# Another order for the attention turns that carry no side products: a difference of scores through ScalarE in place of one maximum in eight

## The chip, the cores and the metric

The kernel runs on one core of a Trainium2 chip. Five engines work side by side on it, each through its own list of instructions in order: TensorE (PE in the profile; its weight loads stand apart as PEld), VectorE (DVE), ScalarE (ACT), GpSimd (POOL) and SyncE (SP), which issues most transfers. Matrix products end in PSUM, eight banks of 128 partitions by 512 numbers; VectorE and ScalarE read them from there. The metric is the time of one execution on the device in microseconds; lower is better.

## What is computed

The reference is a block with a modulated layer norm, attention with 32 query heads that share one key and one value head of 16 columns, and a gated product of two projections without a nonlinearity:

```python
x = A_x
mod = (_silu(c) @ w_mod).reshape(c.shape[0], 6, 1, -1)
sa, ca, ga, sb, cb, gb = (mod[:, 0], mod[:, 1], mod[:, 2], mod[:, 3], mod[:, 4], mod[:, 5])
h = _layernorm(x, axis=-1) * (1 + ca) + sa
q = (h @ wq) in 32 heads of 16; k = h @ wk; v = h @ wv        # one key and one value head
p = _softmax(q @ k.T / 4, axis=-1)
x = x + ga * ((p @ v) @ wo)
h = _layernorm(x, axis=-1) * (1 + cb) + sb
x = x + gb * (((h @ w_gate) * (h @ w_up)) @ w_down)
```

There are 2048 rows of 512 columns, and the gated part is 1792 wide. Everything is float32 outside; inside, products that need it are made of two float16 halves.

## The kernel before

The attention is cut into 32 *units*. A unit is one block of 512 query rows and four heads, so `u = 8 * block + group` (`UB = 8`). For each unit the largest score of every query row is wanted before the exponentials are taken, and so each unit is worked on twice.

*Maxima.* The maxima of unit u are taken while unit u-1 is in its exponentials. They come in 32 slots, each with one product for `a = 0` and one for `a = 1`: 128 queries against 512 of the 2048 keys, into a PSUM tile `mx`. The two values of `a` are two heads that stand in the upper and the lower 64 rows of TensorE's array (48 of the 64 are used), so two such products with different `a` can stream at the same time. VectorE reduces each `mx` to one column of `mpart` (L574). After slot 31 `max_fin` reduces `mpart` to `mm` (L591), TensorE transposes `mm` into `mxt` (L598), ScalarE and VectorE write it as two halves `mt` (L603, L604), and two transfers lay these as two more rows into `sst`, the query operand of the unit. A score that comes out of `sst` and `kst` then already has its maximum taken off.

*Exponentials.* A *turn* is one tile of 128 keys of a unit, 16 turns to a unit. It has four products `sc` (keys by 512 queries, four heads, by `p` and `a`; L621), four exponentials on ScalarE into `P` (L623), and the product P times V of the turn before it (`pv`, L632): four products with 128 rows and 32 columns each, side by side in the array, whose sums stay in one PSUM bank for the whole unit. `P` has eight buffers, two turns' worth.

*PSUM.* All eight banks stand in one queue. `ps_hold` takes the one at the front, `ps_give` puts it at the end, and `ps_mx` and `ps_sc` do both at once. `pv` holds one bank for good, so a tile `mx` or `sc` gets the bank of the seventh tile before it, and its product waits until ScalarE or VectorE has read that tile. Anything else that is placed between turns (the transposes `mxt`, sums of squares of weights at L916, transposes of the second layer norm at L765) takes a bank from the same queue.

*Side products.* Projections of q, the output projection and the gated part are cut into groups of products, and each turn takes some of them in between where a group is ready. `attend` makes two turns and chooses one of three orders for both (written by hand, as strings): `MANY` (eight side products a turn), `FEW` (four a turn, for q) and `NO_SIDE`. In a string, `e0` is a score product with its exponential for `a = 0`, `m1` a maximum for `a = 1`, `x0` a side product. `NO_SIDE` stands where no side product is to be had. By the program these are 31 calls of `attend`, two turns each: 26 in one stretch, from unit 5, turn 6, to unit 8, turn 9, while maxima of units 6 to 9 are taken; and 5 from unit 9, turn 8, to unit 10, turn 1, while the block's second layer norm is made ready (maxima of units 10 and 11).

After the products of a turn `attend` calls `pv` for the turn before. In the middle and at the end of each turn it runs what stands in lists: `late_max` (the transpose of a unit's maxima, a slot after `max_fin`), `hooks` (weight loads, splits and sums of squares; a step of these lists is half a turn), `turns` (the transposes L765), and at the start and in the middle `drain_posts`, the evacuations that belong to what was run before.

*The first unit.* For unit 0, where nothing else keeps VectorE busy, another form of the maximum is there already. Of two 512-key parts a and b, TensorE makes b - a in one bank, as two products (`kng` is a part of the keys with its sign turned); ScalarE takes its positive part into `rel` (L577); then TensorE makes a, and one VectorE instruction adds `rel` and reduces the sum to its maximum (L579, with a short second instruction that reads the accumulator). That is the maximum over both parts.

Of the kernel before, what the change touches and what calls it, by code (L numbers as in the profile page):

```python
# [23 lines left out]
UB = H // 4  # L24
NU = NB * UB
KT = S // 128
# [13 lines left out]

CHANNEL = {0: KC - 1, 3: 0, 4: 1, 6: 2}
LOW = -3.0e38
SYNC = mybir.DependencyInfo(mybir.DependencyClass.Sync, mybir.DependencyReason.DATA)

NO_SIDE = "e0 e1 m0 m1 e0 e1 m0 m1"
FEW = "e1 m0 e0 x1 m0 x1 e0 x1 m0 x1 e1 m0"  # L50
MANY = "x1 e0 x1 m0 x1 e0 x1 e0 x1 m0 x1 m0 x1 m0 x1 e0"

# [2 lines left out]
def adaln_mqa_glu_kernel(ctx: ExitStack, tc: tile.TileContext, x_in, wq_in, wk_in, wv_in, wo_in,  # L55
# [410 lines left out]
    ended = []  # L466
# [72 lines left out]
    def max_slots(u):  # L539


        if u == 0:
            slots = [[[("one", r // 4, r % 4, kc)] for _ in range(2)] for kc in range(2) for r in range(8)]
            for r in range(8):
                for a in range(2):
                    slots[-1][a].append(("diff", r // 4, r % 4, 2))
                slots.append([[("both", r // 4, r % 4, 2)] for _ in range(2)])
            return slots
        return [[[("one", r // 4, r % 4, kc)] for _ in range(2)] for kc in range(4) for r in range(8)]

    flat = [(u, i, last, step) for u in range(NU) for steps in [max_slots(u)]
# [4 lines left out]
    def max_parts(u):  # L556
        if u < NU and u not in mparts:
            mparts[u] = work.tile([128, 2, 2, 4, 4], F32, name="mpart")
            if u == 0:
                nc.vector.memset(mparts[u], LOW)  # L560

    def max_mm(u, a, op):
# [19 lines left out]
    def drain_relus():  # L582
        for f in relus:
            f()
        relus.clear()
# [41 lines left out]
    def pv(u, kt):  # L627
        if kt == 0:
            pvb[u] = ps_hold("pv")
        for j in range(4):  # L630
            p, a = divmod(j, 2)
            nc.tensor.matmul(pvb[u][32 * j:32 * j + 32, :], vst[:, kt, :], ptl[u, kt, p, a],  # L632
                             start=(kt == 0), stop=(kt == KT - 1))
# [413 lines left out]
    def max_half(a):  # L1047
        n = mstep[a]
        mstep[a] += 1
        if n >= len(flat):  # L1050
            return
        u, i, last, ops = flat[n]
        max_parts(u)
        for op in ops[a]:
            max_mm(u, a, op)
        if a == 0:
            return
        if 0 < u < NU - 1 and i == QPRE:
            load_q(u + 1)
        if i == 12:  # L1060
            max_parts(u + 1)
        if last:
            max_fin(u)
            (_, f, g), = max_rows(u)
            later[mstep[1] + 1] = (f, g)

    def late_max():
        for at in [m for m in later if m <= mstep[1]]:
            f, g = later.pop(at)
            f()  # L1070
            posts.append(g)
            return True
        return False
# [61 lines left out]
    def attend(u, kt):  # L1135


        now[0] = u * NSTEP + 2 * kt
        if cur and cur[0].ended():
            cur.clear()  # L1140
        side = cur[0] if cur else fill[0][1] if open_gate(now[0]) else None
        style = NO_SIDE if side is None else FEW if side in qs else MANY
        order = [(w[0], int(w[1])) for w in style.split()]
        count = {}
        for turn in range(2):
            now[0] = u * NSTEP + 2 * (kt + turn)
            sync["before"] = sync["exp"]
            drain_posts()
            for j, (what, a) in enumerate(order):
                if j == len(order) // 2:  # L1150
                    drain_posts()
                    late_max()
                    hooks(u, 2 * (kt + turn))
                a = a if style is NO_SIDE else a ^ turn
                if what == "m" and mstep[a] >= len(flat) and style is MANY:
                    mstep[a] += 1
                    side_half(a, second)
                elif what == "m":
                    max_half(a)
                elif what == "x":  # L1160
                    side_half(a)
                else:
                    k = count[a] = count.get(a, -1) + 1
                    qk_exp(u, kt + (k // 2 if style is MANY else turn), k % 2, a)
            assert not sync["due"]
            for g in ended:
                g.finish()
            ended.clear()
            for f in ends:
                f()  # L1170
            ends.clear()
            v = u * KT + kt + turn - 1
            if v >= 0:
                pv(*divmod(v, KT))
                if v % KT == KT - 1:
                    ends.append(lambda: pv_out(u - 1))
            if not late_max() and turns:
                _, f, post = turns.popleft()
                f()
                posts.append(post)  # L1180
            hooks(u, 2 * (kt + turn) + 1)
# [98 lines left out]
```

## Time and profile before

| what | before |
|---|---|
| time, median of 3 runs | 1682.76 us (1682.55 to 1683.22) |
| the profiled execution: time, span | 1682.67 us, 1680.6 us |
| granted TensorE clock | 0.998 |
| first stretch without side products, 26 pairs of turns | 299.74 to 429.17 us, 129.43 us |
| second stretch, 5 pairs | 470.25 to 499.49 us, 29.24 us |

The two stretches are measured from the start of their first exponential to the start of the first exponential after them; 208 and 40 exponentials lie in them. TensorE, VectorE and ScalarE are busy for 99%, 83% and 72% of the whole span. These shares mix stretches with side products, where TensorE is the limit, and the two without.

### The profile page before, as it was taken

How to read it: one execution, taken by the hardware profiler on the slowest of the kernel's cores; microseconds unless marked ns; L12 is line 12 of the kernel's file. 1: busy time of each engine (PE TensorE's matmuls, PEld its weight loads, DVE VectorE, ACT ScalarE, POOL GpSimd, SP SyncE). 2: the span in 40 equal slices, each digit the busy share in tenths (PEclk: the TensorE clock that was granted, in tenths of full speed). 3: DMA queues.
4: the chain of work that ended last, by engine and by line, in shares of the span. 5: the costliest groups of instructions: out<-in, count | busy, mean ns of one | idle time of the engine just before them, and what ended most of it. 6: DMA issues, size and time to landing. Idle time of an engine off the chain costs nothing.

```text
span 1680.6 us, 33352 instructions
## 1 busy us (share of the span) xinstructions
PE 1656.3 (99%) x12749; PEld 535.4 (32%) x12749; DVE 1390.0 (83%) x2365; ACT 1216.1 (72%) x2288; POOL 518.1 (31%) x690
## 2 busy tenths in 40 slices
PE   8999999999999999999999999999999999999999
PEld 3333333222223333333333333333333333334444
DVE  7999999999989999999989999999998999703110
ACT  5688888888787778777777777877777777772010
POOL 5745354626676740200140211101032111112230
PEclk9999999999999999999999999999999999999999
DMA  6112122211321200001100000000010000001000
GB/s 245 72 40 88 54 88 61 94 48 50 84 66 56 85 22 9 17 10 29 35 15 12 15 15 10 16 10 17 24 32 12 23 16 6 12 5 49 13 1 25
DMA packets 48556, 66.33 MB, mean 39 GB/s; under 512 B 14726, under 2 KB 29194, under 8 KB 48396
## 3 DMA queue, kind: packets, MB, share of 16 engines
q1 hardware_dynamic: 46812, 63.87, 12.2%
q8 instruction: 100, 1.64, 0.4%
q14 instruction: 60, 0.49, 0.1%
q10 hardware_dynamic: 1584, 0.33, 0.1%
HBM read 51.05 MB, written 8.65 MB: 36 GB/s over the span
## 4 chain that ended last, share of the span: by engine, by line
PE 87%; DVE 9%; ACT 2%; DMA 1%; issue 0%; ACTq 0%; DVEq 0%
PE side L485 50%; PE pv L632 27%; DVE mpart L574 8%; PE sc L621 5%; PE mx L570 3%; ACT P L623 2%; PE mx L765 1%; DMA xbig<-in_A_x_dram 1%; PE mxt L598 0%; DVE bs L238 0%; PE sc L570 0%; PE pk L274 0%; DMA wkv<-in_A_wv_dram 0%; DVE rel L579 0%; PE part L267 0%
## 5 line engine op out<-in xcount | busy, mean ns | idle before, releaser
L574 DVE TENSOR_REDUCE mpart<-mx 128x1 f32<-128x512 f32 x2016 | 1266.1, 683 | 91.6 <-PE mx L570 88.3
L623 ACT ACTIVATE P<-sc 128x512 f32<-128x512 f32 x2048 | 1092.0, 599 | 264.6 <-PE sc L621 223.1
L621 PE MATMUL sc<-sst,kst 50*128 50x512 f16 x2048 | 661.0, 379 | 1.0 <-DVE mpart L574 0.8
L570 PE MATMUL mx<-kst,sst 48*128 48x512 f16 x2032 | 617.3, 377 | 6.5 <-DVE mpart L574 3.8
L632 PE MATMUL pv<-P,vst 128*32 128x512 f32 x4096 | 545.3, 605 | 1.2
L485 PE MATMUL side<-h2T,wg 64*128 64x512 f16 (+1 forms) x1168 | 284.3, 378 | 0.1
L485 PE MATMUL side<-h2T,wu 64*128 64x512 f16 (+1 forms) x1166 | 282.9, 378 | 0.1
L485 PE MATMUL side<-wd,glu 64*128 64x512 f16 (+1 forms) x1008 | 234.1, 378 | 0.0
L818 POOL TENSOR_SCALAR glu<-gf 128x512 f16<-128x512 f32 x56 | 34.7, 620 | 617.2 <-DVE gf L817 538.9
L621 PEld LDWEIGHTS <-kst 50*128 50x128 f16 x2048 | 175.2, 94 | 129.4 <-issue 109.6
L570 PEld LDWEIGHTS <-sst 48*128 48x128 f16 x2064 | 183.9, 94 | 58.7 <-issue 37.4
L485 PEld LDWEIGHTS <-wg 64*128 64x128 f16 (+1 forms) x1168 | 100.9, 94 | 202.7 <-ACT P L623 95.0
L485 PEld LDWEIGHTS <-wu 64*128 64x128 f16 (+1 forms) x1166 | 100.8, 95 | 200.2 <-ACT P L623 92.5
L632 PEld LDWEIGHTS pv<-P,vst 128*32 128x32 f32 x4096 | 80.8, 108 | 218.8 <-issue 202.8
L485 PEld LDWEIGHTS <-glu 64*128 64x128 f16 (+1 forms) x1008 | 89.1, 95 | 163.2 <-ACT P L623 63.0
L817 DVE TENSOR_TENSOR gf<-side,g 128x512 f32<-128x512 f32 x56 | 38.3, 684 | 115.8 <-PE side L485 82.5
L485 PE MATMUL side<-h,wq 64*128 64x512 f16 (+1 forms) x349 | 92.5, 376 | 0.0
L812 ACT ACTIVATE g<-side 128x512 f32<-128x512 f32 x56 | 33.2, 593 | 81.5 <-PE side L485 81.5
L485 PE MATMUL side<-wo,och 64*128 64x512 f16 (+1 forms) x336 | 79.3, 378 | 0.0
L819 POOL TENSOR_TENSOR glu<-gf,glu 128x512 f16<-128x512 f32 x56 | 65.0, 1161 | 4.7
L200 POOL TENSOR_SCALAR rv<-st 128x1 f32<-128x1 f32 (+1 forms) x20 | 4.6, 228 | 158.3 <-DVE st L725 143.2
L666 POOL TENSOR_TENSOR oc<-oc,rr 128x512 f32<-128x512 f32 x15 | 19.1, 1275 | 107.4 <-DMA sst<-qd 94.3
(223 smaller groups left out, 810.5 us busy)
## 6 DMA issues: line engine op xcount, KB each, us to landing
wsl<-in_B_w_gate_dram SPq DMA_DIRECT2D x32, 224.0 KB
wsl<-in_B_w_up_dram SPq DMA_DIRECT2D x32, 224.0 KB
wsl<-in_B_w_down_dram SPq DMA_DIRECT2D x28, 256.0 KB
sst<-qd SPq DMA_DIRECT2D x180, 32.0 KB
oc<-ev SPq DMA_DIRECT2D x128, 32.0 KB
rr<-ri SPq DMA_DIRECT2D x16, 256.0 KB
xl<-in_A_x_dram SPq DMA_DIRECT2D x16, 256.0 KB
qd<-q SPq DMA_DIRECT2D x15, 256.0 KB
```

The source lines that it names most:

```text
L485: return nc.tensor.matmul(self.p, left[64 * r0:64 * r1], right[64 * r0:64 * r1], start=start, stop=self.ended())
L570: nc.tensor.matmul(m, s[64 * a:64 * a + 48, p, t * 128:(t + 1) * 128], w[64 * a:64 * a + 48, :], start=(i == 0), stop=(i == len(keys) - 1))
L574: nc.vector.tensor_reduce(part, m, axis=AX.X, op=OP.max)
L621: nc.tensor.matmul(t, kst[64 * a:64 * a + 50, kt * 128:(kt + 1) * 128], s[64 * a:64 * a + 50, p, :], start=True, stop=True)
L623: ex = nc.scalar.activation(ptl[u, kt, p, a], t, AF.Exp)
L632: nc.tensor.matmul(pvb[u][32 * j:32 * j + 32, :], vst[:, kt, :], ptl[u, kt, p, a], start=(kt == 0), stop=(kt == KT - 1))
L666: eng.tensor_tensor(o, o, st["r"], op=OP.mult)
L765: nc.tensor.transpose(st["p"][:, t * 128:(t + 1) * 128], n2s[b, t][:, k * 128:(k + 1) * 128], ident)
L812: nc.scalar.activation(st["g", f], p, AF.Copy, scale=2.0 ** -45)
L817: nc.vector.tensor_tensor(gf, p, st["g", f], op=OP.mult)
L818: nc.gpsimd.tensor_scalar(st["glu"][:, 0, f, :], gf, 1.0, 0.0, op0=OP.mult, op1=OP.add)
L819: nc.gpsimd.tensor_tensor(st["glu"][:, 1, f, :], gf, st["glu"][:, 0, f, :], op=OP.subtract)
```

## The change

Three things change, and all of them in turns of the order `NO_SIDE`.

1. Units 6 to 9 (`DIFFS`) order the slots of their maxima by row instead of by key part, `a = 0` taking the parts in the order 0, 2, 1, 3. In turns without side products, slot 1 of four of `a = 0` becomes a difference (parts 2 and 3, through `kng`), which ScalarE evacuates, and slot 3 becomes the product that takes `rel` along. By the program this happens 26 times, once in each pair of turns of the first stretch: VectorE gets seven tiles where it got eight, ScalarE nine where it got eight, and TensorE makes one product more. The second stretch has no differences.
2. The order is written out over two turns and changes. `a = 0` and `a = 1` no longer alternate, and the first of the two turns takes three maxima of `a = 0`, the second three of `a = 1`. A unit's last slot is therefore done when the slower of both is (`mstep[1 - a]`, `min(mstep)`).
3. `v` in the string is the place of P times V (with what the end of a turn brings, `end_turn`). In the second turn it stands ahead of the last score product.

```diff
+DIFFS = range(UB - 2, UB + 2)
+DIFF_AT, BOTH_AT = 1, 3
...
-NO_SIDE = "e0 e1 m0 m1 e0 e1 m0 m1"
+NO_SIDE = ("m0 m0 e1 m0 e1 e0 m1 e0 v", "e0 m1 m0 m1 e1 m1 e0 v e1")
...
+        if u in DIFFS:
+            order = [0, 1]
+            order[DIFF_AT:DIFF_AT] = [2]
+            order.insert(BOTH_AT, 3)
+            return [[[("one", r // 4, r % 4, kc)] for kc in (order[i], i)] for r in range(8) for i in range(4)]
...
-            if u == 0:
+            if u == 0 or u in DIFFS:
                 nc.vector.memset(mparts[u], LOW)
...
+    def max_half(a, diffs=False):
...
-        for op in ops[a]:
-            max_mm(u, a, op)
-        if a == 0:
+        for kind, p, t, kc in ops[a]:
+            if a == 0 and u in DIFFS and i % 4 == DIFF_AT and diffs:
+                kind, open_diff[0] = "diff", True
+            elif a == 0 and u in DIFFS and i % 4 == BOTH_AT and open_diff[0]:
+                kind, kc, open_diff[0] = "both", 2, False
+            max_mm(u, a, (kind, p, t, kc))
+        if mstep[1 - a] <= n:
             return
...
-            later[mstep[1] + 1] = (f, g)
+            later[min(mstep) + 1] = (f, g)
...
-        for at in [m for m in later if m <= mstep[1]]:
+        for at in [m for m in later if m <= min(mstep)]:
...
+        def end_turn(kt):
+            for g in ended:
+                g.finish()
+            ended.clear()
+            for f in ends:
+                f()
+            ends.clear()
+            v = u * KT + kt - 1
+            if v >= 0:
+                pv(*divmod(v, KT))
+                if v % KT == KT - 1:
+                    ends.append(lambda: pv_out(u - 1))
...
+            order = orders[turn]
...
-                    max_half(a)
+                    max_half(a, style is NO_SIDE)
+                    drain_relus()
+                elif what == "v":
+                    end_turn(kt + turn)
...
-            for g in ended:
-                g.finish()
-            ended.clear()
-            for f in ends:
-                f()
-            ends.clear()
-            v = u * KT + kt + turn - 1
-            if v >= 0:
-                pv(*divmod(v, KT))
-                if v % KT == KT - 1:
-                    ends.append(lambda: pv_out(u - 1))
+            if style is not NO_SIDE:
+                end_turn(kt + turn)
```

Where a pair of turns ends (`sst_128` belongs to the unit in its exponentials, `sst_126` and `sst_127` to units whose maxima are taken; `kwb` holds `kng`). On TensorE, before, around the end of a turn:

```order
L570 LDWEIGHTS sst_126
L570 MATMUL mx<-kst,sst_126 128x512
L632 MATMUL pv<-P,vst 32x512 x4
L621 LDWEIGHTS kst
L621 MATMUL sc<-sst_128,kst 128x512
L621 LDWEIGHTS kst
L621 MATMUL sc<-sst_128,kst 128x512
```

And on TensorE now, around the end of a pair's second turn, with the first products of the next pair:

```order
L628 LDWEIGHTS kst
L628 MATMUL sc<-sst_128,kst 128x512
L639 MATMUL pv<-P,vst 32x512 x4
L628 LDWEIGHTS kst
L628 MATMUL sc<-sst_128,kst 128x512
L577 LDWEIGHTS sst_127
L577 MATMUL mx<-kst,sst_127 128x512
L577 LDWEIGHTS sst_127
L577 MATMUL mx<-kst,sst_127 128x512
L628 LDWEIGHTS kst
L628 MATMUL sc<-sst_128,kst 128x512
```

A turn's last score product now stands behind `pv`, and two maxima follow it where two score products stood.

In the pair in which unit 6's last maxima are taken, TensorE before has this around the transpose `mxt` (the last slot's products stand ahead of the `pv` shown):

```order
L632 MATMUL pv<-P,vst 32x512 x4
L621 LDWEIGHTS kst
L621 MATMUL sc<-sst_128,kst 128x512
L621 LDWEIGHTS kst
L621 MATMUL sc<-sst_128,kst 128x512
L570 LDWEIGHTS sst_127
L570 MATMUL mx<-kst,sst_127 128x512
L570 LDWEIGHTS sst_127
L570 MATMUL mx<-kst,sst_127 128x512
L598 MATMUL mxt<-ident,mm 16x128
L621 LDWEIGHTS kst
L621 MATMUL sc<-sst_128,kst 128x512
```

And now:

```order
L639 MATMUL pv<-P,vst 32x512 x4
L628 LDWEIGHTS kst
L628 MATMUL sc<-sst_128,kst 128x512
L577 LDWEIGHTS sst_126
L577 MATMUL mx<-kst,sst_126 128x512
L577 LDWEIGHTS sst_127
L577 MATMUL sc<-kwb,sst_127 128x512
L577 LDWEIGHTS sst_127
L577 MATMUL sc<-kst,sst_127 128x512
L577 LDWEIGHTS sst_127
L577 MATMUL mx<-kst,sst_127 128x512
L605 MATMUL mxt<-ident,mm 16x128
```

The last slot's product (`mx` of `sst_126`) has moved from ahead of `pv` to behind it, into the same turn as the transpose that needs its reduction.

On ScalarE, before, around the evacuation `mt` of the same transpose:

```order
L638 ACTIVATE ev<-pv,evs 128x512
L623 ACTIVATE P<-sc 128x512 x16
L514 ACTIVATE qf<-side,qvs 128x512
L623 ACTIVATE P<-sc 128x512 x32
L603 ACTIVATE mt_4850<-mxt 16x128
L623 ACTIVATE P<-sc 128x512 x16
```

And now:

```order
L630 ACTIVATE P<-sc 128x512 x8
L584 ACTIVATE rel<-sc 128x512
L630 ACTIVATE P<-sc 128x512 x3
L610 ACTIVATE mt_4860<-mxt 16x128
L630 ACTIVATE P<-sc 128x512 x5
L584 ACTIVATE rel<-sc 128x512
L630 ACTIVATE P<-sc 128x512 x8
```

The positive parts stand one to eight exponentials, and ahead of `mt` are the three exponentials of the second turn, the last of them that of the score product behind `pv`.

More of the change, by code (lines that the diff above doesn't have):

```diff
@@ L1045, in drain_posts @@
             f()
-    def max_half(a):
+    open_diff = [False]
+    def max_half(a, diffs=False):
         n = mstep[a]
@@ L1053, in max_half @@
         max_parts(u)
-        for op in ops[a]:
-            max_mm(u, a, op)
-        if a == 0:
+        for kind, p, t, kc in ops[a]:
[5 more added lines that the diff above has]
+        if mstep[1 - a] <= n:
             return
+        u, i, last, ops = flat[n]
         if 0 < u < NU - 1 and i == QPRE:
@@ L1142, in attend @@
         style = NO_SIDE if side is None else FEW if side in qs else MANY
-        order = [(w[0], int(w[1])) for w in style.split()]
+        orders = [[(w[0], int(w[1:] or 0)) for w in s.split()] for s in (style if style is NO_SIDE else (style, style))]
         count = {}
+        def end_turn(kt):
[10 more added lines that the diff above has]
+                    ends.append(lambda: pv_out(u - 1))
         for turn in range(2):
```

## The prediction

> **What bounds the kernel now.** I first read where the time without side products lies (the table by stretches), then who waits there (the waits), then one turn in order of time, then the first unit, which shows the operations that are added. In the table the columns behind the length are busy time and count of TensorE, its weight loads, VectorE, ScalarE and GpSimd.
>
> ```profile
> core 0: us, PE busy (x) PEld busy (x) DVE busy (x) ACT busy (x) POOL busy (x), PEclk, DMA share, GB/s
> 299.74:429.17 129.43, 122.15 (x874) 30.38 (x872) 128.99 (x231) 109.81 (x215) 67.45 (x78) 1.00 0.21 64
> 470.25:499.49 29.24, 27.28 (x181) 7.15 (x179) 25.49 (x45) 25.88 (x50) 22.13 (x34) 1.00 0.21 63
> 333.89:338.63 4.74, 4.74 (x34) 1.11 (x32) 4.74 (x10) 4.13 (x8) 2.09 (x2) 1.00 0.35 114
> 343.39:348.17 4.78, 4.33 (x34) 1.11 (x32) 4.78 (x9) 4.13 (x8) 4.34 (x5) 1.00 0.11 31
> 394.71:400.32 5.61, 4.57 (x36) 1.03 (x33) 5.58 (x11) 4.38 (x10) 2.47 (x4) 1.00 0.00 0
> ```
>
> ```profile
> ACT P L623 <- PE sc L621: 19.2, 51, 1.1
> PE mx L570 <- DVE mpart L574: 3.8, 17, 0.2
> PE mxt L598 <- DVE mm L591: 1.9, 3, 0.8
> ```
>
> In the first stretch VectorE works 128.99 of 129.43 us. ScalarE waits 19.2 us for scores, TensorE 3.8 us for banks that VectorE has not read: both follow VectorE. A pair of turns with nothing else in it takes 4.74 to 4.78 us (the two short windows); I take 4.76. One turn:
>
> ```profile
> 339.72 12.63 DVE L574 TENSOR_REDUCE mpart<-mx 128x1 f32<-128x512 f32 x21
> ...
> 340.58 0.39 PE L621 MATMUL sc<-sst,kst 50*128 50x512 f16 x2
> ...
> 340.81 0.38 PE L570 MATMUL mx<-kst,sst 48*128 48x512 f16 x2
> ...
> 341.01 2.06 ACT L623 ACTIVATE P<-sc 128x512 f32<-128x512 f32 x4 [0.31 <-PE sc L621]
> 341.03 0.39 PE L621 MATMUL sc<-sst,kst 50*128 50x512 f16 x2
> ...
> 341.64 0.39 PE L570 MATMUL mx<-kst,sst 48*128 48x512 f16 x2 [0.23 <-DVE mpart L574]
> ...
> 341.97 1.06 PE L632 MATMUL pv<-P,vst 128*32 128x512 f32 x8
> 342.96 0.10 PEld L621 LDWEIGHTS <-kst 50*128 50x128 f16 x2 [0.84 <-issue]
> ```
>
> From it: a reduce every 0.60 us ((12.63 - 0.68) / 20), eight of them 4.78 us, which is the pair. An exponential every 0.49 us ((2.06 - 0.60) / 3). Two products of the two halves start together, and the next two 0.22 us later (340.58, 340.81, 341.03). From the last of them to `pv` it is 0.31 us (341.64 to 341.97, the second of the two a hundredth or two later), from `pv` to the next score 1.00. From a score product's start to its exponential 0.43 us. Three more delays, at places where the reader sat idle:
>
> ```profile
> 486.19 0.38 PE L570 MATMUL mx<-kst,sst 48*128 48x512 f16 x2
> ...
> 486.61 2.48 DVE L574 TENSOR_REDUCE mpart<-mx 128x1 f32<-128x512 f32 x4 [0.76 <-PE mx L570]
> ...
> 492.77 0.78 ACT L772 ACTIVATE hf<-mx,hsc 128x512 f32<-128x512 f32 x1 [0.67 <-PE mx L765]
> ...
> 493.60 0.86 PE L570 MATMUL mx<-kst,sst 48*128 48x512 f16 x2 [0.19 <-ACT hf L772]
> ```
>
> Product to reduce 0.42 us; end of the reader to the next product in its bank 0.05 (493.55 to 493.60).
>
> **The added operations** run in the first unit, before the exponentials begin:
>
> ```profile
> 57.66 0.68 DVE L579 CUSTOM_DVE_ANT_0 rel<-mx,rel 128x512 f32<-128x512 f32 x1
> 58.27 0.08 DVE L579 DVE_READ_ACCUMULATOR2_ANT mpart<- 128x1 f32 x1
> 58.27 0.69 DVE L579 CUSTOM_DVE_ANT_0 rel<-mx,rel 128x512 f32<-128x512 f32 x1
> ```
>
> ```profile
> L577 ACT ACTIVATE rel<-sc 128x512 f32<-128x512 f32 x16 | 8.4, 608 | 3.7 <-PE mx L570 2.8 <-PE sc L570 0.7
> ```
>
> The joint reduce comes every 0.61 us, its second instruction hidden inside; the positive part takes 0.61 us alone, like an exponential's 0.60, so I give it the same 0.49 in a chain.
>
> **A plain pair, now.** VectorE: 6 x 0.60 + 0.61 = 4.21 us. ScalarE: 9 x 0.49 = 4.41. TensorE without any wait: the longer row half takes four further steps of 0.22 behind the first product in each turn, so twice 0.88 + 0.31 + 1.00 = 4.38. None of the three reaches 4.76, but banks come back only after seven tiles. I follow one pair from T = 0, where the last `e1` of the pair before and the first `m0` start behind `pv`. `both` and `e1` start at 0.22, `m0` and `e1` at 0.44, `e0` at 0.66. `m1` is the seventh tile after that last `e1`, whose exponential starts at 0.43, takes 0.60 and frees the bank at 1.08; `m1` would have been ready at 0.66. The last `e0` needs the bank of the first `m0`: 0.42 + 0.68 + 0.05 = 1.15, where 0.88 would do. `pv` at 1.46, second turn at 2.46. There `e0` and `m1` start at once, the difference's two products 0.22 and 0.44 later, `e1` at 0.66, the last `m1` and `e0` at 0.88; every bank there has been free for 0.3 us or more. `pv` at 1.19, the next pair at 2.19. Sum 4.65 us: the limit passes from VectorE to TensorE and the banks, and 0.11 of the 0.55 us taken off VectorE comes through. Over 26 pairs: **-2.9 us**. Bounds: 4.38 (no bank wait, -9.9) and 4.76 (0).
>
> **VectorE's other work in the stretch** is on the limit today:
>
> ```profile
> L574 DVE TENSOR_REDUCE mpart<-mx 128x1 f32<-128x512 f32 x209 | 126.6, 677 | 0.3 <-PE mx L570 0.2
> L940 DVE TENSOR_REDUCE gm<-gbb 128x1 f32<-128x512 f32 x1 | 0.7, 662 | 0.0
> L591 DVE TENSOR_REDUCE mm<-mpart 128x16 f32<-128x64 f32 x3 | 0.7, 220 | 0.1
> ```
>
> 128.99 - 126.6 = 2.4 us, of which some 1.0 belongs to the unit ends (next). The rest, 1.4, now falls into 0.44 us a pair that VectorE has to spare; the two 0.66 reduces stick out by a little. **-1.1** (0 to -1.4).
>
> **Unit ends.** Three lie in the stretch. Before, one of them:
>
> ```profile
> 397.73 0.22 DVE L591 TENSOR_REDUCE mm<-mpart 128x16 f32<-128x64 f32 x1
> ...
> 398.10 0.27 PE L598 MATMUL mxt<-ident,mm 128*16 128x128 f32 x1 [0.81 <-DVE mm L591]
> 398.30 0.39 PE L621 MATMUL sc<-sst,kst 50*128 50x512 f16 x2
> ...
> 399.75 0.25 ACT L603 ACTIVATE mt<-mxt 16x128 f16<-16x128 f32 x1
> ...
> 400.26 0.27 DVE L604 SCALAR_TENSOR_TENSOR mt<-mxt,mt 16x128 f16<-16x128 f32 x1
> ...
> 400.48 3.72 DVE L574 TENSOR_REDUCE mpart<-mx 128x1 f32<-128x512 f32 x6
> ```
>
> TensorE waits 0.81 us for `mm`, and the pair takes 5.61 (another takes 0.2 less): about 0.75 over the plain one. Now the last slot's product stands in the turn of the transpose itself. It starts with the second turn, 2.46; its reduce runs from 2.88 to 3.56, `mm` to 3.80, `mxt` starts 0.15 later at 3.95 and the next score at 4.15, where 3.12 was due: 1.03 us. Then, in the next pair, ScalarE's `mt` queues behind the exponential of the score behind `pv`: it starts at 0.43 + 0.49 = 0.92, VectorE's `mt` at 1.22, and the pair's first reduce behind it at 1.44 in place of 0.42. The last `e0` of that turn waits for exactly this bank: another 1.02. Behind both stand `pv`, and so all. 2.05 now against 0.75: **+3.9** over three (0 if the stalls are covered as before, +5). The transfers of `mt` start about 1.5 us later in the turn; before, 3.9 us lay between the second one and the unit's first score, and the stalled pair is longer by as much, so I cost that at nothing.
>
> **Between the turns.** Four sums of squares (L916) and two small products of the weights' scales fall into the stretch:
>
> ```profile
> 352.41 0.40 PE L916 MATMUL mx<-kwb,onec 128*32 128x128 f32 x8
> 352.75 0.39 PE L621 MATMUL sc<-sst,kst 50*128 50x512 f16 x2
> ```
>
> Each takes 0.34 us of TensorE and a bank. A pair without one spares TensorE 0.38 us today (4.76 - 4.38) and nothing now. Behind the first turn such an item costs 0.3 either way; behind the second, a score stands between `pv` and it, and I add 0.2 for leaving and entering the row halves once more (2 x 0.09, the 0.31 above less 0.22). Three such: **+0.6** (0 to +2). [...] The evacuations of `pv` (three, 0.6 us of ScalarE) find 0.24 us spare a pair and stuck out by 0.2 before too: 0.
>
> **Second stretch.** No differences: VectorE keeps eight reduces, 4.78, and sits idle 0.06 at a pair's start, where the first maximum is only 0.42 behind `pv`: 5 x 0.08 = +0.4. One unit end, VectorE with more in its queue: +1.1. The four transposes, where VectorE idles 0.76 us a turn, may go either way: 0 (-1 to +1). **+1.5**.
>
> GpSimd's and SyncE's lists keep their order; GpSimd is busy 67.45 of 129.43 us, so a changed pace finds it with room. Turns with side products differ in the slots' parts alone, at no cost: TensorE limits them.
>
> **Sum.** -2.9 - 1.1 + 3.9 + 0.6 + 1.5 = +2.0 us on the profiled execution's 1682.67 (span 1680.6, 2.1 around it; the median of the runs is 1682.76): **1684.7 us**, no change that a measurement can tell (0.2% is 3.4 us). What the sum says: the gain is spent at the unit ends.
>
> **Rivals.** *Faster: banks come back in time.* If `m1` and the last `e0` are not held up, a plain pair takes 4.38 to 4.5 us, 4 to 7 us less than in my sum, and the time is 1678 to 1681; with the second stall at unit ends hidden too, 1675. For it: all three engines' sums lie below 4.41. Against: today's 0.23 us before each second pair of maxima is the same wait. It is faster by 0.2% from 0.21 us a pair below my 4.65. 0.20.
>
> *Slower: the two row halves don't overlap freely.* Today both halves start together in every step of these turns; now they start at different steps and next to others. If a product had to wait for its neighbour in the other half at two places of a pair, 0.22 us each, the pair would take 5.09 and the time is 1684.7 + 26 x 0.44 = 1696; 0.06 us a pair is enough for slower by 0.2%. Against it, in a turn with side products the halves start 0.1 us apart and keep their step (the maximum and the score are of one half, 0.23 us apart):
>
> ```profile
> 604.14 0.37 PE L570 MATMUL mx<-kst,sst 48*128 48x512 f16 x1
> ...
> 604.27 0.38 PE L485 MATMUL side<-h2T,wg 64*128 64x512 f16 x1
> 604.37 0.37 PE L621 MATMUL sc<-sst,kst 50*128 50x512 f16 x1
> ```
>
> Small delays of this kind, or unit ends at their bound of +5, are the likelier part of it: 0.32, most of it below 1690.
>
> *Table loads.* Were ScalarE to load its tables at each change between exponential and positive part, 52 loads at 1.28 us would give 1751.
>
> ```profile
> 2.29 1.28 ACT L179 ACT_TABLE_LOAD   x1 [2.29 <-issue]
> ```
>
> The one load of the program stands ahead of the first unit's positive parts and all exponentials: 0.01. [...]
>
> *It does nothing:* a transfer or GpSimd sets the time behind the stretch, 1682.8: inside my own case.
>
> **Chances and range.** My forecast, with "it does nothing" in it, 0.47; faster 0.20; slower 0.33. The range reaches into both: 1678.5 (plain pair 4.41) to 1690.5 (pair 4.85, or unit ends and items at their upper bounds).
>
> **What would show it.** In the changed kernel: plain pairs near 4.65 us with TensorE never idle for long and VectorE idle 0.4 us a pair; waits of TensorE for exponentials and reduces of some 0.3 us a pair in place of ScalarE's for scores; `mxt` waiting about 1 us for `mm`; pairs at unit ends near 5.7, twice running. Wrong if plain pairs stay at 4.76 or go below 4.5, if `mt` does not wait, or if the stretch behind 429 us shifts by another amount than these two stretches gain or lose.

## The result, and the profile after

The changed kernel takes 1680.66 us (median of 22 runs, 1679.79 to 1681.68); the kernel before, run beside it, 1683.27 (22 runs, 1682.00 to 1684.17). The ratio is 0.9986 with a 95% interval of 0.9980 to 0.9992: 2.6 us faster, a small gain where the prediction had a small loss (1684.7; its range, 1678.5 to 1690.5, holds the time). The interval leaves out 1, so the gain, though small, is there.

The table by stretches of the kernel after: the first stretch, the second, a plain pair of turns, the two pairs of a unit's end, a pair with an evacuation of `pv`. The columns are those of the prediction's first table.

```profile
300.22:427.81 127.59, 121.00 (x901) 31.56 (x900) 118.17 (x232) 119.70 (x240) 68.01 (x78) 1.00 0.22 65
468.84:498.10 29.26, 27.13 (x182) 7.45 (x182) 25.55 (x45) 26.04 (x49) 21.77 (x34) 1.00 0.22 63
389.20:393.67 4.47, 4.39 (x34) 1.17 (x33) 4.38 (x9) 4.47 (x10) 4.22 (x5) 1.00 0.06 23
393.67:399.68 6.01, 4.89 (x35) 1.12 (x34) 4.24 (x9) 4.89 (x12) 2.43 (x4) 1.00 0.01 3
399.68:404.92 5.24, 4.93 (x34) 1.26 (x34) 5.03 (x10) 4.46 (x10) 1.09 (x2) 1.00 0.44 131
404.92:409.96 5.04, 4.67 (x34) 1.20 (x33) 4.79 (x10) 5.04 (x11) 4.62 (x8) 1.00 0.01 2
```

VectorE falls from 128.99 to 118.17 us in the first stretch, ScalarE rises from 109.81 to 119.70, and the stretch is 1.84 us shorter. A plain pair takes 4.47 us, 0.29 less than the 4.76 before, and ScalarE is busy in all of it. The two pairs of a unit's end take 11.25 us where the same end took 10.35 before, 5.61 (in the prediction's table) and behind it:

```profile
400.32:405.06 4.74, 4.73 (x34) 1.11 (x32) 4.74 (x10) 4.13 (x8) 1.07 (x2) 1.00 0.47 148
```

The waits of the first stretch after, in the same view as before:

```profile
ACT P L630 <- PE mx L577: 4.7, 10, 0.9
DVE mt L611 <- ACT mt L610: 4.4, 3, 1.5
```

ScalarE's waits of exponentials for products, 19.2 us in one row before, are down to 4.7 in their largest row, and a new wait of VectorE has come: for `mt`, three times 1.5 us, at the three unit ends.

By kind of pair, from the starts of each pair's first exponential in both traces (us, after less before; "predicted" is worked out from the prediction's terms: 0.11 less in each of the 26 pairs, and what was put on top for its kind):

| pairs | count | measured | predicted |
|---|---|---|---|
| plain | 13 | -3.70 | -1.4 (13 x -0.11) |
| unit ends, two each | 6 | +3.18 | +3.2 (3.9 - 6 x 0.11) |
| with an evacuation of `pv` | 3 | +0.18 | -0.3 |
| with VectorE's other work and most of the items between turns | 4 | -1.52 | -0.9 (-1.1 - 0.4 + 0.6) |
| first stretch | 26 | -1.86 | +0.5 (-2.9 - 1.1 + 3.9 + 0.6) |
| second stretch | 5 | +0.02 | +1.5 |

The pair ahead of the first stretch is 0.25 us longer, and the pairs at the other borders of the two stretches add -0.2. Outside of these places the two profiled executions differ by 0.2 us ahead of the change and 0.4 behind it. In the kernels below, this offset ahead of the change was anywhere from 0 to 1.2 us, so it says nothing of the change.

One plain pair of the kernel after, TensorE in order of time, and one reduce of VectorE that a score waits for:

```profile
388.28 0.39 PE L628 MATMUL sc<-sst,kst 50*128 50x512 f16 x1
...
388.74 0.69 DVE L581 TENSOR_REDUCE mpart<-mx 128x1 f32<-128x512 f32 x1
...
389.40 0.37 PE L577 MATMUL mx<-kst,sst 48*128 48x512 f16 x1
389.48 0.37 PE L628 MATMUL sc<-sst,kst 50*128 50x512 f16 x1
389.79 1.07 PE L639 MATMUL pv<-P,vst 128*32 128x512 f32 x8
390.79 0.39 PE L628 MATMUL sc<-sst,kst 50*128 50x512 f16 x1
390.79 0.39 PE L577 MATMUL mx<-kst,sst 48*128 48x512 f16 x1
391.01 0.38 PE L577 MATMUL sc<-kwb,sst 48*128 48x512 f16 x1
391.01 0.38 PE L577 MATMUL mx<-kst,sst 48*128 48x512 f16 x1
391.23 0.38 PE L628 MATMUL sc<-sst,kst 50*128 50x512 f16 x1
391.23 0.37 PE L577 MATMUL sc<-kst,sst 48*128 48x512 f16 x1
391.44 0.38 PE L628 MATMUL sc<-sst,kst 50*128 50x512 f16 x1
391.45 0.38 PE L577 MATMUL mx<-kst,sst 48*128 48x512 f16 x1
391.76 1.07 PE L639 MATMUL pv<-P,vst 128*32 128x512 f32 x8
392.75 0.39 PE L628 MATMUL sc<-sst,kst 50*128 50x512 f16 x1
```

The first turn is as forecast. Its last maximum stands back until 389.40 and its last score until 389.48. The maximum starts 0.05 us behind the end of the exponential that has read its bank (388.72 to 389.35), the score 0.05 us behind the end of the reduce that has read its own (388.74 and 0.69). Then comes `pv`, and the second turn starts 2.51 us after the first (forecast: 2.46). The second turn takes 1.96 us where 2.19 was forecast. In the program the maximum at 391.01 stands behind both products of the difference (`kwb`, then `kst`), yet it starts 0.22 us ahead of the second of them (391.23). So each row half goes through its own four steps, 0.22 us apart, and neither waits for the other.

A unit's end after (all engines):

```profile
396.44 0.22 DVE L598 TENSOR_REDUCE mm<-mpart 128x16 f32<-128x64 f32 x1
...
396.81 0.27 PE L605 MATMUL mxt<-ident,mm 128*16 128x128 f32 x1 [0.73 <-DVE mm L598]
...
399.52 0.25 ACT L610 ACTIVATE mt<-mxt 16x128 f16<-16x128 f32 x1
...
399.80 0.28 DVE L611 SCALAR_TENSOR_TENSOR mt<-mxt,mt 16x128 f16<-16x128 f32 x1 [1.46 <-ACT mt L610]
```

Both forecast stalls are there. TensorE stands 0.73 us for `mm` (0.81 before, some 1 us forecast). Then VectorE stands 1.46 us, with the next pair's reduces behind, for the `mt` that ScalarE reaches only behind its exponentials (399.52, 2.7 us behind the transpose).

### The profile page after: what moved, and what is told of

The parts are those of the page before. It is cut to its first block, busy times and chain, and to the rows that moved or that the text cites. A ratio compares the mean times of both kernels' runs of the same rounds, so it can differ in the third digit from the quotient of the medians.

```text
span 1678.6 us, 33368 instructions
## 1 busy us (share of the span) xinstructions
PE 1655.8 (99%) x12775; PEld 537.8 (32%) x12775; DVE 1379.6 (82%) x2369; ACT 1225.9 (73%) x2314; POOL 518.1 (31%) x690
## 4 chain that ended last, share of the span: by engine, by line
PE 90%; DVE 5%; ACT 4%; DMA 1%; issue 1%; ACTq 0%; DVEq 0%
PE side L487 50%; PE pv L639 28%; PE sc L628 6%; PE mx L577 3%; DVE mpart L581 3%; ACT P L630 3%; PE mx L772 1%; PE sc L577 1%; DMA xbig<-in_A_x_dram 0%; PE mxt L605 0%; DVE bs L240 0%; ACT rel L584 0%; DVE rel L586 0%; PE part L269 0%; DMA wkv<-in_A_wv_dram 0%
## 5 line engine op out<-in xcount | busy, mean ns | idle before, releaser
L581 DVE TENSOR_REDUCE mpart<-mx 128x1 f32<-128x512 f32 x1964 | 1241.1, 683 | 94.0 <-PE mx L577 87.6
L628 PE MATMUL sc<-sst,kst 50*128 50x512 f16 x2048 | 686.2, 378 | 3.6 <-DVE mpart L581 1.8
L577 PE MATMUL mx<-kst,sst 48*128 48x512 f16 x2006 | 625.1, 377 | 2.8 <-DVE sst L291 0.3
L628 PEld LDWEIGHTS <-kst 50*128 50x128 f16 x2048 | 182.6, 94 | 142.3 <-issue 122.8
```

The costliest lines, as they stand in the source:

```text
L577: nc.tensor.matmul(m, s[64 * a:64 * a + 48, p, t * 128:(t + 1) * 128], w[64 * a:64 * a + 48, :], start=(i == 0), stop=(i == len(keys) - 1))
L581: nc.vector.tensor_reduce(part, m, axis=AX.X, op=OP.max)
L628: nc.tensor.matmul(t, kst[64 * a:64 * a + 50, kt * 128:(kt + 1) * 128], s[64 * a:64 * a + 50, p, :], start=True, stop=True)
```

## The experiments

All kernels are the changed kernel with one edit unless said otherwise. "Plain pair" is read from the starts of the first exponentials of successive pairs, away from unit ends, evacuations and items. The kernel before ran again beside each of them, and each ratio is to those runs.

**Parts alone.** First the differences without the new order: every turn's products as before the change.

```diff
-NO_SIDE = ("m0 m0 e1 m0 e1 e0 m1 e0 v", "e0 m1 m0 m1 e1 m1 e0 v e1")
+NO_SIDE = ("e0 e1 m0 m1 e0 e1 m0 m1 v",) * 2
```

> Differences and positive parts as in the changed kernel, but the products of every turn in the old order (scores, maxima, scores, maxima, then P times V). Theory one, the difference alone makes the gain: VectorE 4.21 us a pair, ScalarE 4.41, TensorE with free row halves 1.97 + 2.19 and one bank wait of some 0.35 behind the positive part; a plain pair takes 4.5 us (4.41 to 4.6), unit ends cost what they cost before (0.75 over a plain pair), and the time is 4 to 5 us under the kernel before, so below the changed kernel. Theory two, the new order is needed for the banks to come back in time: plain pairs at 4.65 us or more, and the time is at or above the changed kernel's.

Measured: 1683.91 us, ratio to the kernel before 1.0006 (0.9997 to 1.0015): no gain. A plain pair takes 4.82 us. The table by stretches (a plain pair), the waits in the first stretch, and TensorE in that pair:

```profile
390.75:395.57 4.82, 4.72 (x36) 1.02 (x33) 4.33 (x8) 4.51 (x11) 4.59 (x5) 1.00 0.01 4
```

```profile
DVE mpart L581 <- PE mx L577: 10.2, 24, 0.7
ACT P L630 <- PE sc L628: 9.7, 29, 0.6
```

```profile
390.96 0.85 PE L577 MATMUL mx<-kst,sst 48*128 48x512 f16 x2
...
393.19 0.38 PE L628 MATMUL sc<-sst,kst 50*128 50x512 f16 x2
393.49 0.37 PE L577 MATMUL sc<-kwb,sst 48*128 48x512 f16 x1
...
393.81 0.37 PE L577 MATMUL mx<-kst,sst 48*128 48x512 f16 x1
```

VectorE and ScalarE now both wait for products, and TensorE for banks: of the two maxima at 390.96 the second starts 0.48 us after the first instead of beside it (0.85 less 0.37), and the difference starts at 393.49, 0.30 behind the scores instead of 0.22, when VectorE gives its bank back. What ends last in both turns is one wait: the last maximum takes the bank of the turn's own first score. In the second turn shown that score starts at 392.74, its exponential runs from 393.16 to 393.76, and the maximum starts at 393.81. With the delays of the prediction this wait alone makes a turn of 0.43 + 0.60 + 0.05 + 0.31 + 1.00 = 2.39 us and a pair of 4.78, whatever VectorE does. It was there before the change too (in the turn that the prediction shows, the first score's exponential ends at 341.60 and the second of the last two maxima starts at 341.65), level with VectorE's own 4.78, so "both follow VectorE" was half of it. So "theory one" falls and "theory two" holds: VectorE's relief alone goes straight into waits for banks.

Then the new order without differences:

```diff
-DIFFS = range(UB - 2, UB + 2)
+DIFFS = range(0)
```

> The new order of products and the new place of P times V, without differences (every maximum read by VectorE). Theory one: VectorE again has eight reduces of 0.60 us a pair, so plain pairs are at 4.78 to 4.9 us; unit ends cost 2.0 us as in the changed kernel, 1 us more than before each; the time is 2 to 5 us above the kernel before. Theory two, the order itself frees time: plain pairs below 4.74 and a time at or under the kernel before.

Measured: 1690.92 us (four runs, one of them 1695.43), 1.0052 (1.0039 to 1.0066), 7.7 us above the kernel before. A plain pair:

```profile
396.45:401.35 4.90, 4.76 (x32) 1.03 (x32) 4.88 (x10) 4.17 (x10) 4.68 (x5) 1.00 0.00 0
```

The plain pair is at 4.90, at the upper end expected, with VectorE busy in 4.88 of it. The total is above the expected 2 to 5: unit ends cost 1.2 to 1.5 us more than before (I expected 1), and the four pairs with VectorE's other work lose 1.8 us, since all of it lies on the limit again.

Last, `v` alone put back to the second turn's end:

```diff
-NO_SIDE = ("m0 m0 e1 m0 e1 e0 m1 e0 v", "e0 m1 m0 m1 e1 m1 e0 v e1")
+NO_SIDE = ("m0 m0 e1 m0 e1 e0 m1 e0 v", "e0 m1 m0 m1 e1 m1 e0 e1 v")
```

> The changed kernel with P times V back at the second turn's end: its last score (e1) stands ahead of it, all else as in the changed kernel. Worked out with row halves that start products freely, signals in program order and seven banks (0.22 us a step, 0.42 to the reader, 0.49 and 0.60 between readers): that half has five steps, P times V comes 0.22 us later, and the score's exponential queues behind four others; the next turn's P times V waits for it. A plain pair takes 4.85 us, so the place of P times V is worth 0.4 us a pair and the time is some 8 to 10 us above the changed kernel's. If the place is worth nothing, plain pairs stay at 4.47 to 4.5; if only the step counts, 4.69.

Measured: 1685.97 us, 1.0017 (1.0008 to 1.0027) against the kernel before, 5.3 us above the changed kernel (expected: 8 to 10); a plain pair takes 4.90 (expected: 4.85). The expected total took the 0.4 us for every pair of the stretch; the thirteen plain pairs give 4.8 us, and the unit ends are 0.7 us shorter than the changed kernel's.

So neither the differences (+0.7 us, not told from nothing) nor the order (+7.7) gains anything by itself, nor do both without the new place of `pv` (+2.6); all together gain 2.6. The place of `pv` alone was not run.

**Do the row halves run as two lanes?** The second turn with all of the upper half's products ahead of the lower half's in the program; each half keeps its own order.

```diff
-NO_SIDE = ("m0 m0 e1 m0 e1 e0 m1 e0 v", "e0 m1 m0 m1 e1 m1 e0 v e1")
+NO_SIDE = ("m0 m0 e1 m0 e1 e0 m1 e0 v", "e0 m0 e0 m1 m1 e1 m1 v e1")
```

> The changed kernel with the second turn's products in another program order: all of the upper row half (score, the difference's two, score) ahead of those of the lower one (maximum, maximum, score, maximum); each half's own order stays. If products start in program order across the halves, as the prediction had it, the first maximum of the lower half can't start before the last score of the upper one, 0.66 us into the turn: the second turn takes 2.63 us and a plain pair 5.13, in place of 4.47 in the changed kernel. If each row half is a lane of its own that starts its products as they come, the second turn stays at 1.97 and a plain pair at 4.47 (4.41 to 4.55). If a product can pass one that waits for the other half, but only one, 4.91. The transpose of a unit's end comes to stand behind the turn's last score, so unit ends are not compared here.

Measured: 1685.5 us (one run), plain pairs 4.94 to 4.99 us and two of 5.15: on average none of the three numbers. The second turn in order of time:

```profile
394.60 0.39 PE L628 MATMUL sc<-sst,kst 50*128 50x512 f16 x1
...
394.61 0.39 PE L577 MATMUL mx<-kst,sst 48*128 48x512 f16 x1
...
395.04 0.37 PE L577 MATMUL sc<-kst,sst 48*128 48x512 f16 x1
...
395.10 0.53 PE L628 MATMUL sc<-sst,kst 50*128 50x512 f16 x2
...
395.62 1.06 PE L639 MATMUL pv<-P,vst 128*32 128x512 f32 x8
395.71 1.89 DVE L581 TENSOR_REDUCE mpart<-mx 128x1 f32<-128x512 f32 x3 [0.66 <-PE mx L577]
...
396.62 0.39 PE L628 MATMUL sc<-sst,kst 50*128 50x512 f16 x1
```

The products do run as lanes: the lower half's first maximum starts at 394.61, beside the first score, though four products of the upper half stand ahead of it in the program, three of which have yet to start, and the turn takes 2.02 us, not 2.63. But its reduce starts at 395.71, 1.10 us behind its product instead of 0.42. It starts 0.08 us behind the end of the upper half's last score (the second of the two at 395.10, which end at 395.63), the last product ahead of the maximum in the program. It is the same in each of the 26 pairs of the stretch: 0.88 us behind the difference's first product each time. So in this run products start out of order between the halves, and their readers are let go in order. The three reduces then end late, their banks come back late, and the first turns wait: 2.93 us (4.95 less 2.02) in a pair of 4.95, where it was 2.51.

To see whether the reader really hangs on the products ahead of its own, one of them is moved behind it (the edit is to the kernel just shown):

```diff
-NO_SIDE = ("m0 m0 e1 m0 e1 e0 m1 e0 v", "e0 m0 e0 m1 m1 e1 m1 v e1")
+NO_SIDE = ("m0 m0 e1 m0 e1 e0 m1 e0 v", "e0 m0 m1 e0 m1 e1 m1 v e1")
```

> As in the run with the upper half's products ahead, but the first maximum of the lower half stands ahead of the upper half's last score: score, difference (two), maximum, score, maximum, lower score, maximum. The products should start at the same moments as in that run (0.22 us apart in each half). If a reader is let go only when every product ahead of its own in program order is done, the first reduce of the second turn now starts behind the difference's second product instead of behind the last score: 0.65 us behind the difference's first product in place of 0.88, and a plain pair takes 4.70 us on average in place of 4.95 to 5.15. If the reader only waits for its own product and something else held that reduce up, it stays at 0.88; with readers free altogether it would be 0.43, and the pair 4.48.

Measured: 1682.92 us (one run), plain pairs 4.73 to 4.93 (4.70 on average expected).

```profile
392.85 0.39 PE L577 MATMUL mx<-kst,sst 48*128 48x512 f16 x1
393.07 0.38 PE L577 MATMUL sc<-kwb,sst 48*128 48x512 f16 x1
...
393.29 0.37 PE L577 MATMUL sc<-kst,sst 48*128 48x512 f16 x1
...
393.73 1.89 DVE L581 TENSOR_REDUCE mpart<-mx 128x1 f32<-128x512 f32 x3 [0.43 <-PE sc L628]
```

The maximum starts with the turn again, and its reduce at 393.73: 0.66 us behind the difference's first product (0.65 expected, 0.88 in the run above), 0.07 behind the end of its second. It is 0.66 or 0.67 in 25 of the 26 pairs; in the other one VectorE was busy until then. The first section has each engine work through its list in order. In these two runs the readers follow that order (they start 0.08 and 0.07 us behind the end of the last product ahead of their own); the starts don't, between the two row halves: one came ahead of up to three products that stand before it (394.61 ahead of 394.82, 395.04 and the score behind them).

**Are banks what holds the first turn?** One of the seven banks is put aside for the length of the stretch.

```diff
+    aside = []
...
+        if (u, kt) == (5, 6):
+            aside.append(pool.popleft())
+        if (u, kt) == (8, 10):
+            pool.append(aside.pop())
```

> The changed kernel with one PSUM bank put aside from the stretch's first pair of turns to its last: tiles rotate through six banks instead of seven, the instructions and their order are the same. If the return of banks sets the first turn (its last maximum waits for the exponential of the last e1, its last score for the reduce of the first m0, each now one tile nearer), plain pairs go from 4.47 to about 5.45 us and the whole stretch gets 20 to 27 us longer. If ScalarE's nine readers (4.41 us) set the pair and banks are only touched, plain pairs stay below 4.7.

Measured: 1704.34 us (one run); the stretch is 23.9 us longer, a plain pair takes 5.48.

```profile
300.16:451.61 151.45, 135.39 (x901) 30.29 (x899) 119.04 (x232) 123.11 (x240) 70.11 (x81) 0.99 0.18 54
404.83:410.31 5.48, 4.91 (x33) 1.09 (x33) 4.38 (x9) 4.62 (x10) 4.45 (x6) 1.00 0.00 0
```

The instructions are the same, each engine has idle time, and the pair is 1.0 us longer. The size (5.45 expected) agrees with how the first turn's waits were worked out: with six banks they set the pair. With seven they hold up the last two products of the first turn, as the plain pair after shows.

**Unit ends.** The transpose is moved from the middle of the second turn to behind `pv`, and its two copies to directly behind it, ahead of the last score's exponential:

```diff
-            later[min(mstep) + 1] = (f, g)
+            later[min(mstep) + 1 + diffs] = (f, g)
...
                 if v % KT == KT - 1:
                     ends.append(lambda: pv_out(u - 1))
+            if style is NO_SIDE and late_max():
+                posts.pop()()
```

> The changed kernel, but in turns without side products the transpose of a unit's maxima stands behind P times V of the turn instead of in its middle, and its two copies (ScalarE's and VectorE's mt) are issued right behind it, ahead of the exponential of the turn's last score. If the two stalls at a unit's end are the wait of the transpose for mm and the queue of mt behind that exponential, the pairs at unit ends go from 6.0 to 4.7..5.0 us and from 5.24 to 4.5..4.7, three times: 4 to 5.5 us less in the first stretch, up to 1 in the second, 1675 to 1677 us. If the stalls only move (the transpose's bank and the two copies delay the next turn's products as long as before), less than 1.5 us comes off, and the pairs still add to over 10.5 us.

Measured: 1674.50 us, ratio to the kernel before 0.9949 (0.9936 to 0.9961): 6.2 us under the changed kernel and 8.8 under the kernel before. The two stretches, then the two pairs of a unit's end:

```profile
300.35:422.67 122.32, 119.25 (x901) 31.56 (x900) 118.10 (x232) 119.26 (x240) 68.02 (x79) 1.00 0.23 67
463.69:491.99 28.30, 27.12 (x182) 7.51 (x182) 25.57 (x45) 26.14 (x50) 21.73 (x34) 1.00 0.22 65
...
390.38:395.12 4.74, 4.66 (x35) 1.25 (x34) 4.60 (x11) 4.74 (x11) 2.39 (x4) 1.00 0.02 3
395.12:399.77 4.65, 4.65 (x34) 1.17 (x33) 4.56 (x9) 4.46 (x10) 1.05 (x2) 1.00 0.48 148
```

6.01 and 5.24 have become 4.74 and 4.65; the first stretch is 5.3 us shorter than the changed kernel's, the second 1.0. The stalls did not move elsewhere. Each half of the edit alone tells whether there were two of them. Only the transpose (the copies where they were):

```diff
-            later[min(mstep) + 1] = (f, g)
+            later[min(mstep) + 1 + diffs] = (f, g)
...
+            if style is NO_SIDE:
+                late_max()
```

> Only the first half of moving the unit end: the transpose stands behind P times V in the second turn, its copies are issued at the next turn's start as in the changed kernel, behind the exponential of the last score. If the first stall is the wait of the transpose for mm and the second is mt behind that exponential, the first pair of a unit end falls from 6.0 to 4.7..4.9 us and the second stays at 5.2 to 5.4: 3 to 4 us under the changed kernel. If both stalls are one and the same, the second falls too, and the time is that of both moved, 1674.5.

Measured: 1677.46 us, 0.9965 (0.9952 to 0.9978), 3.2 under the changed kernel. Only the copies (the transpose where it was; `tops` holds what `late_max` has just put up):

```diff
+    tops = []
...
+            tops.append(g)
...
+            while style is NO_SIDE and tops:
+                g = tops.pop()
+                if g in posts:
+                    posts.remove(g)
+                    g()
```

> Only the second half: the transpose stays in the middle of the second turn, its copies are issued behind P times V, ahead of the exponential of the last score. By the same theory the first pair of a unit end stays at 6.0 us and the second falls from 5.24 to 4.65: 1.5 to 2.5 us under the changed kernel. If the second stall is something else, the second pair stays above 5.1.

Measured: 1677.88 us, 0.9968 (0.9957 to 0.9979), 2.8 under it. The same unit end in both, first with the transpose moved, then with the copies moved:

```profile
392.44:397.34 4.90, 4.55 (x35) 1.17 (x34) 4.14 (x9) 4.79 (x12) 4.57 (x7) 1.00 0.01 3
397.34:402.58 5.24, 4.93 (x34) 1.26 (x34) 5.03 (x10) 4.46 (x11) 1.20 (x3) 1.00 0.30 89
```

```profile
391.91:397.75 5.84, 5.03 (x35) 1.21 (x34) 5.00 (x11) 4.86 (x11) 2.42 (x4) 1.00 0.01 3
397.75:402.17 4.42, 4.33 (x34) 1.17 (x33) 4.33 (x9) 4.42 (x11) 1.10 (x2) 1.00 0.52 158
```

Each edit takes away one stall and leaves the other, and 3.2 and 2.8 add to 6.0 of the 6.2: two stalls, as the prediction had them. Their sizes differ more than forecast (1.03 and 1.02): the first edit takes 1.11 us off the first pair (6.01 to 4.90), the second 0.82 off the second (5.24 to 4.42).

**Is ScalarE the next bound?** On top of the moved unit ends, VectorE takes over the evacuation of `pv` in turns without side products.

```diff
+        plain[0] = style is NO_SIDE
...
-        nc.scalar.activation(ev, pvb[u], AF.Copy, scale=evs)
+        if plain[0]:
+            nc.vector.tensor_scalar(ev, pvb[u], evs, None, op0=OP.mult)
+        else:
+            nc.scalar.activation(ev, pvb[u], AF.Copy, scale=evs)
```

> The kernel with the unit end moved, and in turns without side products the evacuation of P times V is done by VectorE instead of ScalarE. If ScalarE now bounds a pair (nine readers, 4.41 us; with the evacuation's 0.6 it is 5.0, and these pairs take 5.04), the three pairs with an evacuation in the first stretch go to VectorE's sum, 4.21 + 0.6 = 4.8, and the time is 0.5 to 1 us under the kernel with the unit end moved alone, about 1673.8. If VectorE's reduces are what holds the banks of the next products, the pairs stay at 5.0 or get longer.

Measured: 1676.86 us, 0.9963 (0.9949 to 0.9977): 2.4 us over the kernel with only the unit ends moved (2.8 when each is taken against the runs beside it), where 0.5 to 1 less was expected. First the pair in which VectorE reduces the weights' scales, then a pair with an evacuation and the one behind it:

```profile
367.09:373.50 6.41, 5.34 (x40) 1.52 (x39) 6.01 (x15) 4.74 (x10) 0.32 (x1) 1.00 0.36 106
```

```profile
401.41:406.10 4.69, 4.43 (x34) 1.06 (x33) 4.68 (x10) 4.62 (x10) 4.36 (x7) 1.00 0.00 0
406.10:410.84 4.74, 4.72 (x34) 1.22 (x35) 4.65 (x9) 4.47 (x11) 1.28 (x2) 1.00 0.23 56
```

The first part of the theory holds (with only the unit ends moved the pair took 5.05, now 4.69), but the pair behind gives it back (4.41 to 4.74): over both it is 9.43 against 9.46 us, no gain. Where VectorE has other work it loses: the pair behind the second evacuation takes 6.41 us in place of 5.40. So relief of ScalarE brings nothing here. The 2.4 us are not all accounted for: of 2.2 us between the two profiled executions, 0.8 lie in the first stretch, the rest ahead of it and behind the second, where the two kernels do the same.

## Why the prediction was wrong

**The failed step** is the second turn of the plain pair: "the difference's two products 0.22 and 0.44 later, `e1` at 0.66, the last `m1` and `e0` at 0.88", `pv` at 1.19. This working lets a product start only when all ahead of it in the program have started, also those of the other row half. The trace shows the last ones at 0.66 and `pv` at 0.97: 0.22 us less, and a pair of 4.47 instead of 4.65, below the 4.5 that the prediction itself had named as a sign of being wrong. In the thirteen plain pairs this is 2.3 us, as much as the whole difference in the first stretch between +0.5 predicted and -1.8 measured (the evacuations and VectorE's other work, below, were also off, by about as much in opposite directions). The run with the upper half's products ahead shows the step apart: in that order the prediction's rule would give a turn of 2.63 us, and it took 2.02. The prediction's 4.38 us for TensorE without any wait has the same error: with three further steps in the second turn it is 2.19 + 1.97 = 4.16. Put into the prediction's own sum, 4.47 for 4.65 in each of the 26 pairs turns +2.0 into -2.7. That this meets the measured -2.6 is luck: against so short a pair the unit ends and evacuations come out above their terms, and the second stretch below its own, by about as much.

**The first turn** was right (2.51 us for 2.46), with both bank waits at their places; putting one bank aside lengthened the pair as the same working gives it. The limit passed from VectorE as said, but with the pair at 4.47 ScalarE is full as well (busy for 4.47 of 4.47): the prediction's 4.41 for ScalarE lay under its 4.65 and was taken for slack. Which of the two would hold the pair without the other is not shown.

**Unit ends** were right in mechanism and nearly in size: two stalls, 11.25 us for the pairs where 9.30 + 2.05 was forecast. Against the shorter plain pair they cost 2.3 us each, not 2.05, so that the +3.2 in the table fits by luck: shorter plain pairs and longer stalls offset each other. Taking the stalls away gave 6.2 us.

**VectorE's other work** gave 1.5 us (1.1 forecast) in its four pairs, with the items between turns among them; +0.6 for the items can't be told apart from it. That term stands on a slip: the 4.38 us from which TensorE's spare time before the change was taken belongs to the new order; the old one has four steps a turn in each half, which makes 2 x (0.66 + 0.31 + 1.00) = 3.94. An item's 0.34 us fits into the spare time either way. The 0.09 us a change in the 0.6 is the author's estimate, from the 0.31 and the 0.22 us of one turn; no run measures it.

**The evacuations** were costed at nothing, and their three pairs came out 0.5 us above the forecast for them: the evacuation is ScalarE's, which is busy for all of the 5.04 us of such a pair.

**The second stretch** was forecast at +1.5 and came out at 0.0. By pairs it is +0.78, -0.48, +0.50, -0.42 and -0.36 us. The unit end lies in the third pair and was there (moving it took 0.96 off that pair), so the other pairs came out below the forecast. Part of it lies between the four transposes, put at 0 with a bound of -1: from the first to the last it is 9.37 us (484.66 to 494.03) where it was 10.01 (485.38 to 495.39). Why is not shown. The new order alone, without differences, gives the same 29.26 us, so the differences have no part in it.

**The rivals.** "Banks come back in time" gave the right numbers, 4.38 to 4.5 us a pair and 1678 to 1681, by a wrong mechanism: the banks hold up the first turn as forecast. "The row halves don't overlap freely" is the opposite of what happened for starts; for readers it is true in part, and costs 0.5 us a pair where the order brings it out. Table loads: the kernel after has one, as before, 1.28 us at 2.30, and the positive parts of the first stretch take 0.59 us on average.

## What to carry to other kernels

When work is moved from one engine to another under a fixed ring of buffers, first follow the buffers: here relief of VectorE was worth nothing in the old order (4.82 us a pair) and 0.29 us a pair in an order made for seven banks. A gain spread over many turns is easily eaten at the few places where the same order puts a producer's reader too close behind it; those places are worth looking for by their waits (0.7 and 1.5 us here), and two short edits there brought more than the change itself. Products of one row half started here past up to three of the other half that stood ahead in the program, but their readers waited for those (up to 1.10 us from their product's start in place of 0.42): where the order between the halves is free, put products whose readers are urgent ahead in the program.

## What was not expected of the hardware

In the two runs that reorder the second turn, matmuls on separate row halves of TensorE started by the steps of their own half (0.21 to 0.27 us apart in the turns shown), past up to three products of the other half that stand ahead in the program (394.61 beside 394.60, with 394.82, 395.04 and a score behind that one passed), but what waited for a product was let go only when those ahead of it were done: 1.10 us after its start with three passed (394.61 to 395.71), 0.88 with two (392.85 to 393.73), 0.42 with none (486.19 to 486.61 in the kernel before). The readers start 0.08 and 0.07 us behind the end of the last product that stands ahead in the program. How the chip does it the runs do not show.
